# GpSimd sums replanned at their traced length, six weight units as plain float32 products, two additions a pair in batch 1

## The chip, the cores and the metric

The kernel runs on one core of one Trainium2 chip. The metric is the device time of that core in microseconds (us), the median of several runs. One profiled execution of the same program gives the trace from which the rows below come.

## The reference

Softcapped attention over 4 batches, 12 heads, 448 positions and 64 dimensions is followed by two feed-forward networks over the 4 x 448 tokens:

```
scores = cap * tanh((q @ k.T / 8) / cap);  attn = exp(scores - max) / (sum(exp) + 1e-9)
x = (attn @ v) with the heads side by side              # 1792 x 768
h = x @ w_in;  g = 0 if h <= -1, h if h >= 1, else (h + 1)^2 / 4    # 768 -> 2048
y = g @ w_out                                           # 2048 -> 768
out = max(y @ w1, y @ w2, y @ w3) @ w_out2              # 768 -> 768 -> 768
```

The weights come as float64 and are turned into float32 on the chip.

## The kernel before

The work is cut by batch (4) and, in the attention, by pair of heads (6 pairs, `NP`). A pair has 4 chunks (`NCH`) of 112 keys. For each chunk TensorE makes the scores (`score`, L425), ScalarE the tanh (L432); VectorE takes the maximum over the four chunks, GpSimd the maximum over the partitions (`reduce`, L453), VectorE subtracts it from each chunk, ScalarE takes exp (L471), and TensorE multiplies the chunks with v (`weigh`, L619) into the bank `pa`. The sum of the exponentials is formed in one of three ways:

- batch 0: `total` (L485), float32 products of each chunk with ones on TensorE, in four steps a pair;
- batch 1 (`FOURS`): `total4` (L499), for each of the four chunks four products with a 32-column stationary of ones side by side, each over half the columns (224);
- batches 2 and 3 (`POOLED`): three additions a pair on VectorE into `se`, then one GpSimd `partition_all_reduce` into `sb` (L534).

The reciprocal of the sums is taken on 8 partitions: `gather` sends the row into `rc` by a DMA from ScalarE's queue (L575), VectorE inverts, and two DMAs from SyncE's queue spread it into `rs` (only the last pair of batch 0 inverts in place, L607). Then VectorE multiplies: `xf` = `pa` * `rs`. `xf` is split into a high part (L252 or L254) and a rest (L257), both float32r, in the tile `x`.

The feed-forward networks take 64 weight units of 128 x 768 (w_in, w123, w_o2) or 128 x 512 (w_out), in groups that accumulate in a bank `ps_m`. In batch 0 `fetch_first` loads a unit as float64 words into `raw`, and VectorE (L333, L346) and ScalarE (L340) make the float32 unit `wf`, which is stored to DRAM; later batches load it from there (L366). `weights` splits `wf` into high part and rest in `w`. Each product of a 128 x 128 block with a 128 x 448 activation is three float32r matmuls in `parts` (L667 high*high, L668 high*rest, L669 rest*high).

No order is written by hand. Each operation gets a cost for each engine that can do it, a due time (`want`), and the buffers that it uses and takes. `Plan` then runs all of it through a list scheduler and emits each engine's instructions in the order of that plan; the costs are the planner's own and no measurement. Operations of TensorE have a `kind`: a change of kind costs `TURN` = 0.1 and the kind in use is preferred by `STAY` = 3. When a GpSimd operation is planned, VectorE is held for `SHARE` = 1.4. A buffer pool hands out its slots in the order of the due times: `wf` 4, `w` 4, `raw` 3, `h` 9 (for `rs`, `xf` and the tiles of the networks), PSUM banks `m` 3 (`ps_m`, the sums `pr`, and `pa` for the odd pairs of batch 0) and `a` 1. The attention of batch b+1 has due times spread over the networks of batch b, so both are interleaved.

The lines that the change touches most:

```python
PART, SCORE, STEP, SUM = 0.609, 0.8, 0.755, 0.39
ar = op({"P": 2.95}, reduce, w, [m0], [mx], [mb])
ep = op({"P": 2.95}, reduce_sum, begin + 10 + 7 * gap, [sm], [se], [sb])
r = op({"A": 0.6}, gather, w + 0.05, [ep], [src], [rc])
```

Of the kernel before, what the change touches and what calls it, by code (L numbers as in the profile page):

```python
# [20 lines left out]
class Plan:  # L21
# [43 lines left out]
    def run(self):  # L65
# [39 lines left out]
        while left:  # L105
            moved = True
            while moved:
                moved = False
                ts = [o for o in ready if o.kind and at[id(o)] <= t + 1e-9 and can_take(o)]
                turn = min(ts, key=first) if ts else None  # L110

                only = dict.fromkeys(free_at, 0.0)
                for o in ready:
                    if len(o.cost) == 1 and at[id(o)] <= t + 1e-9:
                        e = next(iter(o.cost))
                        only[e] += o.cost[e]
                for o in ready:
                    if at[id(o)] > t + 1e-9 or o.kind and o is not turn:
                        continue
                    idle = [e for e in o.cost if free_at[e] <= t + 1e-9]  # L120
                    if not idle:
                        continue
                    e = next(iter(o.cost))
                    if len(o.cost) > 1:
                        ends = {e: max(free_at[e], t) + only[e] + c for e, c in o.cost.items()}
                        e = min(ends, key=ends.get)
                    if e not in idle or not can_take(o):
                        continue
                    for b in o.takes:
                        free[b.pool] -= 1  # L130
                        queue[b.pool].remove(id(b))
                    c = o.cost[e]
                    if o.kind:
                        c += self.TURN if o.kind != last else 0.0
                        last = o.kind
                    if e == "P":
                        free_at["D"] = max(free_at["D"], t) + self.SHARE
                        heapq.heappush(events, (free_at["D"], serial, None))
                        serial += 1
                    if e == "Q":  # L140

                        free_at[e] = t + c
                        o.t0, o.t1 = t, t + c + 3.2
                    else:
                        free_at[e] = t + c
                        o.t0, o.t1 = t, t + c
                    o.e = e
                    ready.remove(o)
                    done.append(o)
                    heapq.heappush(events, (o.t1, serial, o))  # L150
                    heapq.heappush(events, (free_at[e], serial + 1, None))
                    serial += 2
                    left -= 1
                    moved = True
                    break
            if not left:
                break
            if not events:
                raise RuntimeError("the plan is stuck")
            t = max(t, events[0][0])  # L160
            while events and events[0][0] <= t + 1e-9:
                _, _, o = heapq.heappop(events)
                if o is None:
                    continue
                for b in o.uses:
                    b.users -= 1
                    if not b.users:
                        free[b.pool] += 1
                for x in o.out:
                    x.n -= 1  # L170
                    if not x.n:
                        r = max(
                            d.t1 + (0.0 if d.e in x.cost and len(x.cost) == 1 else self.LATENCY)
                            for d in x.deps
                        )
                        if "Q" in x.cost and x.takes:
                            r = max(r, x.want - self.AHEAD)
                        at[id(x)] = r
                        ready.append(x)
                        serial += 1  # L180
                        heapq.heappush(events, (r, serial, None))
                ready.sort(key=lambda o: key[id(o)])
# [12 lines left out]
def kernel(  # L195
# [23 lines left out]
    NF = w_in.shape[0]  # L219
    NM = w123.shape[1]  # L220
    WU = w_in.shape[2]
    FOURS, POOLED = (1,), (2, 3)

    def pool(name, bufs, **kw):
        return ctx.enter_context(tc.tile_pool(name=name, bufs=bufs, **kw))
# [9 lines left out]
    def buf(p, name, shape, dtype=F32):  # L235
        return plan.buf(p, lambda: pools[p].tile(shape, dtype, tag=p, name=name))
# [133 lines left out]
    def weights(b, i, want):  # L370

        n = width[i]
        wf, got = (fetch_first if b == 0 else fetch_again)(i, want)
        w = buf("w", "w", [P, 2, WU], F32R)
        hi = op(
            c_copy(n / 1000),
            lambda e: copy(e, w.tile[:, 0, :n], wf.tile[:, :n]),
            want - 9, [got], [wf], [w],
        )
        lo = op(  # L380
            c_tt(n / 1000),
            lambda e: tt(
                e, w.tile[:, 1, :n], wf.tile[:, :n], f32(w.tile[:, 0, :n]), ALU.subtract
            ),
            want - 8, [got, hi], [wf, w],
        )
        return w, [hi, lo]


    def attention(b, i, begin, last):  # L390
# [113 lines left out]
            return fn  # L504

        w = begin + 9 + 6 * gap
        if fours or first:
            g = Group(NCH)
            sums = [
                op({"T": SUM if fours else STEP}, (total4 if fours else total)(t[c], g),  # L510
                   w + 0.1 * c, [exps[c]], [t[c], pr], [pr] if c == 0 else [],
                   "sums" if fours else "columns")
                for c in range(NCH)
            ]
            for c in range(1, NCH):
                sums[c].deps.append(sums[0])
        else:
            se = unit("se", rows=C)
            sm = op(
                c_tt(2 * KS),  # L520
                lambda e: tt(e, se.tile, t[0].tile, t[1].tile, ALU.add),
                w, exps[:2], [t[0], t[1]], [se],
            )
            for c in range(2, NCH):
                sm = op(
                    c_tt(2 * KS),
                    lambda e, c=c: tt(e, se.tile, se.tile, t[c].tile, ALU.add),
                    w + 0.1, [sm, exps[c]], [se, t[c]],
                )
            if pooled:  # L530
                sb = unit("sb", rows=C)

                def reduce_sum(e):
                    nc.gpsimd.partition_all_reduce(  # L534
                        out_ap=sb.tile.rearrange("p h s -> p (h s)"),
                        in_ap=se.tile.rearrange("p h s -> p (h s)"),
                        channels=C, reduce_op=bass.bass_isa.ReduceOp.add,
                    )

                ep = op({"P": 2.95}, reduce_sum, begin + 10 + 7 * gap, [sm], [se], [sb])  # L540
            else:
                sums = [op(
                    {"T": STEP}, total(se, Group(1)), begin + 10.9 + 8 * gap, [sm], [se],
                    [pr], "columns",
                )]
        w = begin + 10 + 8.2 * gap

        cols = S // 2 if fours else S
# [14 lines left out]
        if small:  # L563
# [5 lines left out]
            def gather(e):  # L569
                if pooled:  # L570
                    src = sb.tile[0:1].rearrange("p h (c q) -> p (h c) q", q=C)
                else:
                    step = 32 if fours else D
                    src = rs.tile[0:P:step, :cols].rearrange("p (c q) -> p c q", q=C)
                nc.scalar.dma_start(out=rc.tile, in_=src)  # L575

            def spread(e):
                nc.sync.dma_start(out=back, in_=rc.tile)
# [6 lines left out]
                    )  # L585

            src = sb if pooled else rs
            r = op({"A": 0.6}, gather, w + 0.05, [ep], [src], [rc])
            r = op({"S": 3.0 if first else 5.0}, lambda e: None, w + 0.06, [r], [rc, src])

            def turn_over(e):
# [23 lines left out]
        def weigh(c):  # L615
# [10 lines left out]


        avs = [op(
            {"T": STEP}, weigh(0), w, [vl] + (exps[:1] if first else exps + ([] if pooled else sums)),
            [t[0], vt], [pa], "columns",  # L630
        )]
        for c in range(1, NCH):
# [15 lines left out]
            lambda e: tt(e, x.tile[:, 1], xf.tile, f32(x.tile[:, 0]), ALU.subtract),  # L648
            w + 1, [a, hi], [xf, x],
        )  # L650
        return x, [hi, lo]


    def sl(m):
# [1 line left out]

    def parts(pos, want, w, srcs, first, count, ps, g, take):

        wt, wops = w
        done = []  # L660
        for j in range(count):
            a, aops = srcs[first + j]

            def fn(e, j=j, a=a):
                start, stop = g.flags()
                wh, wl = wt.tile[:, 0][:, sl(j)], wt.tile[:, 1][:, sl(j)]
                nc.tensor.matmul(ps.tile[:, :S], wh, a.tile[:, 0], start=start, stop=False)  # L667
                nc.tensor.matmul(ps.tile[:, :S], wh, a.tile[:, 1], start=False, stop=False)  # L668
                nc.tensor.matmul(ps.tile[:, :S], wl, a.tile[:, 0], start=False, stop=stop)  # L669

            o = op(
                {"T": PART}, fn, want(pos + j), [*aops, *wops], [wt, a, ps],
                [ps] if take and j == 0 else [], "layer",
            )
            done.append(o)
        return done
# [176 lines left out]
```

## Time and profile before

| what | value |
|---|---|
| median of 3 runs | 1052.28 us (1052.06 to 1053.23) |
| the profiled execution | 1049.13 us |
| its span, first to last instruction | 1047.3 us |
| TensorE matmuls busy | 1027.1 us, 98% |
| VectorE busy | 812.3 us, 78% |
| ScalarE busy | 508.2 us, 49% |
| GpSimd busy | 154.2 us, 15% |
| mean granted TensorE clock | 0.998 |

Busy time is the union of an engine's instructions; matmuls overlap, each with a tail behind its streaming, so the step from one start to the next is the time that a matmul costs, and the duration in its row is longer. A time in square brackets at the end of a timeline row is how long the engine was idle before it, and who ended the wait.

### The profile page before, as it was taken

The numbers are of one execution on the slowest core, as the hardware profiler recorded it, in microseconds if no ns is written. First come the engines' busy times: TensorE is split into PE (matmuls) and PEld (weight loads), VectorE is DVE, ScalarE is ACT, GpSimd is POOL, SyncE is SP. The second block draws the span as 40 slices with busy tenths as digits, with TensorE's granted clock in tenths as the row PEclk, the third lists the DMA queues.
The fourth block names the chain that finished last, engine by engine and source line by source line (L and its number), as shares of the span: only waits on it lengthen the run. The fifth ranks groups of instructions, "written<-read, shape, count | busy, mean of one in ns | idle before, by whom it ended". The sixth has DMA issues, their size and how long they took to land.

```text
span 1047.3 us, 14331 instructions
## 1 busy us (share of the span) xinstructions
PE 1027.1 (98%) x5472; PEld 813.3 (78%) x5472; DVE 812.3 (78%) x1066; ACT 508.2 (49%) x738; POOL 154.2 (15%) x40
## 2 busy tenths in 40 slices
PE   7988999999999999999999999999999999999998
PEld 2237787787888878878877888788788799999997
DVE  5999999898994889868877589777788578655552
ACT  6887996674571856423523377525235144200101
POOL 2321012011010122132222031231221200000000
PEclk9999999999999999999999999999999999999999
DMA  7339879889885332444234423335432432234331
GB/s 162 123 105 295 280 226 295 290 299 302 285 290 187 99 116 68 119 136 148 96 106 132 146 91 92 108 99 157 126 107 84 143 117 95 91 115 136 106 106 53
DMA packets 66783, 160.53 MB, mean 153 GB/s; under 512 B 8218, under 2 KB 25754, under 8 KB 66714
## 3 DMA queue, kind: packets, MB, share of 16 engines
q1 hardware_dynamic: 66256, 159.53, 48.2%
q8 instruction: 43, 0.70, 0.3%
q14 instruction: 26, 0.21, 0.1%
q10 hardware_dynamic: 458, 0.08, 0.0%
HBM read 131.89 MB, written 27.61 MB: 152 GB/s over the span
## 4 chain that ended last, share of the span: by engine, by line
PE 79%; DVE 7%; DMA 4%; ACT 3%; issue 3%; POOL 3%; SPq 1%; ACTq 0%; POOLq 0%; DVEq 0%
PE ps_m L667 23%; PE ps_m L669 22%; PE ps_m L668 22%; PE ps_s L425 5%; PE ps_a L619 5%; DVE t L257 2%; POOL mb L453 2%; POOL sb L534 1%; DVE mx L257 1%; DMA qk<-in_qk 1%; DVE w L257 1%; PE ps_r L499 1%; ACT t L471 1%; DVE h L750 1%; DMA wf<-w 1%
## 5 line engine op out<-in xcount | busy, mean ns | idle before, releaser
L257 DVE TENSOR_TENSOR w<-wf,w 128x768 fp32r<-128x768 f32 (+1 forms) x256 | 257.1, 1006 | 8.1 <-ACT w L252 4.5
L667 PE MATMUL ps_m<-y,w 128*128 128x448 f32 x432 | 160.4, 371 | 0.0
L254 DVE CAST w<-wf 128x768 fp32r<-128x768 f32 (+1 forms) x120 | 62.5, 521 | 125.2 <-PE ps_m L669 118.7
L668 PE MATMUL ps_m<-y,w 128*128 128x448 f32 x432 | 158.3, 366 | 0.0
L669 PE MATMUL ps_m<-y,w 128*128 128x448 f32 x432 | 158.3, 366 | 0.0
L453 POOL PARTITION_ALL_REDUCE mb<-mx x24 | 79.3, 3306 | 532.7 <-DVE mx L257 424.0
L669 PE MATMUL ps_m<-x,w 128*128 128x448 f32 x384 | 141.4, 368 | 2.9 <-DVE w L257 2.9
L252 ACT ACTIVATE w<-wf 128x768 fp32r<-128x768 f32 (+1 forms) x136 | 101.9, 752 | 86.3 <-PE ps_m L669 60.7
L667 PE MATMUL ps_m<-x,w 128*128 128x448 f32 x384 | 142.8, 372 | 0.0
L667 PE MATMUL ps_m<-g,w 128*128 128x448 f32 x384 | 142.5, 371 | 0.0
L668 PE MATMUL ps_m<-x,w 128*128 128x448 f32 x384 | 141.1, 367 | 0.0
L669 PE MATMUL ps_m<-g,w 128*128 128x448 f32 x384 | 140.5, 366 | 0.0
L668 PE MATMUL ps_m<-g,w 128*128 128x448 f32 x384 | 140.5, 366 | 0.0
L432 ACT ACTIVATE t<-ps_s,qscale 112x896 f32<-112x896 f32 x96 | 92.2, 1003 | 41.9 <-PE ps_s L425 41.9
L471 ACT ACTIVATE t<-t,cap_sb 112x896 f32<-112x896 f32 x96 | 96.5, 1037 | 23.8 <-DVE t L257 23.5
L257 DVE TENSOR_TENSOR t<-t,mb 112x896 f32<-112x896 f32 x96 | 100.1, 1080 | 6.7 <-POOL mb L453 6.7
L667 PEld LDWEIGHTS ps_m<-y,w 128*128 128x128 f32 x432 | 81.1, 188 | 20.3 <-issue 13.4
L425 PE MATMUL ps_s<-qk 64*48 64x448 f32 (+1 forms) x768 | 88.1, 562 | 6.8 <-DMA qk<-in_qk 4.5
L534 POOL PARTITION_ALL_REDUCE sb<-se x12 | 74.7, 6223 | 130.6 <-DVE se L257 118.4
L667 PEld LDWEIGHTS ps_m<-g,w 128*128 128x128 f32 x384 | 72.1, 188 | 18.8 <-issue 10.6
L669 PEld LDWEIGHTS ps_m<-y,w 128*128 128x128 f32 x432 | 81.1, 188 | 7.1
L668 PEld LDWEIGHTS ps_m<-y,w 128*128 128x128 f32 x432 | 81.2, 188 | 6.9
(60 smaller groups left out, 1464.5 us busy)
## 6 DMA issues: line engine op xcount, KB each, us to landing
wf<-w SPq DMA_DIRECT2D x120, 384.0 KB
wf<-w SPq DMA_DIRECT2D x72, 256.0 KB
w<-wf SPq DMA_DIRECT2D x40, 384.0 KB
raw<-in_w SPq DMA_DIRECT2D x18, 768.0 KB
raw<-in_w_in SPq DMA_DIRECT2D x16, 768.0 KB
raw<-in_w_out SPq DMA_DIRECT2D x24, 512.0 KB
qk<-in_qk SPq DMA_DIRECT2D x48, 224.0 KB
w<-wf SPq DMA_DIRECT2D x24, 256.0 KB
```

The lines of the kernel that those rows point to most:

```text
L252: nc.scalar.activation(out=out_, in_=in_, func=AF.Copy)
L254: nc.vector.tensor_copy(out_, in_)
L257: nc.vector.tensor_tensor(out=out_, in0=a, in1=b, op=o)
L425: nc.tensor.matmul(ps.tile[k : k + n, j, :S], qkt.tile[o, 1, c * C + k : c * C + k + n], qkt.tile[o, 0], start=True, stop=True,)
L432: nc.scalar.activation(out=t[c].tile, in_=ps.tile[:C, :, :S], func=AF.Tanh, scale=qscale[:C])
L453: nc.gpsimd.partition_all_reduce(out_ap=mb.tile.rearrange("p h s -> p (h s)"), in_ap=mx.tile.rearrange("p h s -> p (h s)"), channels=C, re ...
L471: lambda e, c=c: nc.scalar.activation(out=t[c].tile, in_=t[c].tile, func=AF.Exp, scale=cap_sb[:C]),
L534: nc.gpsimd.partition_all_reduce(out_ap=sb.tile.rearrange("p h s -> p (h s)"), in_ap=se.tile.rearrange("p h s -> p (h s)"), channels=C, re ...
L619: nc.tensor.matmul(pa.tile[j * D : (j + 1) * D, :S], vt.tile[:, j, c], t[c].tile[:, j], start=start, stop=stop,)
L667: nc.tensor.matmul(ps.tile[:, :S], wh, a.tile[:, 0], start=start, stop=False)
L668: nc.tensor.matmul(ps.tile[:, :S], wh, a.tile[:, 1], start=False, stop=False)
L669: nc.tensor.matmul(ps.tile[:, :S], wl, a.tile[:, 0], start=False, stop=stop)
```

## The change

Four edits. The planner is told that a GpSimd sum takes 6.1 (before 2.95), and `SHARE` is scaled with the length of the GpSimd operation. In batch 0 the first six units of w_in (`PLAIN`) are not split: each product is one float32 matmul of `wf` with `xf`, with a kind and a cost of its own. In batch 1 VectorE adds the chunks by twos (two additions a pair), and `total4` runs over two tiles in place of four. In batches 2 and 3 the DMA of `gather` is issued from SyncE's queue in place of ScalarE's. The due time of the sums in batch 1 moves from `begin + 9 + 6 * gap` to `begin + 10.9 + 8 * gap`.

```diff
-                        free_at["D"] = max(free_at["D"], t) + self.SHARE
+                        free_at["D"] = max(free_at["D"], t) + self.SHARE * c / 3
...
-    FOURS, POOLED = (1,), (2, 3)
+    PLAIN = 6
+    ADDED, FOURS, POOLED = (0, 2, 3, 3), (1,), (2, 3)
...
         wf, got = (fetch_first if b == 0 else fetch_again)(i, want)
+        if b == 0 and i < PLAIN:
+            return wf, [got], True
         w = buf("w", "w", [P, 2, WU], F32R)
...
-        if fours or first:
-            g = Group(NCH)
-            sums = [
-                op({"T": SUM if fours else STEP}, (total4 if fours else total)(t[c], g),
-                   w + 0.1 * c, [exps[c]], [t[c], pr], [pr] if c == 0 else [],
-                   "sums" if fours else "columns")
-                for c in range(NCH)
-            ]
+        if ADDED[b] == 0:
+            srcs = list(zip(t, exps))
+        elif ADDED[b] == 2:
+            srcs = []
+            for c in (0, 2):
+                se = unit("se", rows=C)
+                srcs.append((se, add(t[c], t[c + 1], se, w, exps[c : c + 2])))
         else:
...
-                ep = op({"P": 2.95}, reduce_sum, begin + 10 + 7 * gap, [sm], [se], [sb])
+            ep = op({"P": 6.1}, reduce_sum, begin + 10 + 7 * gap, [sm], [se], [sb])
+        else:
+            g = Group(len(srcs))
+            sums = [
+                op({"T": SUM if fours else STEP}, (total4 if fours else total)(x, g),
+                   (w if first else begin + 10.9 + 8 * gap) + 0.1 * c, [d], [x, pr],
+                   [pr] if c == 0 else [], "sums" if fours else "columns")
+                for c, (x, d) in enumerate(srcs)
+            ]
...
-                nc.scalar.dma_start(out=rc.tile, in_=src)
+                (nc.sync if pooled else nc.scalar).dma_start(out=rc.tile, in_=src)
...
-            r = op({"A": 0.6}, gather, w + 0.05, [ep], [src], [rc])
+            r = op({"Q": 0.1} if pooled else {"A": 0.6}, gather, w + 0.05, [ep], [src], [rc])
...
+            if plain:
+                a, aop = srcs[first + j][2:]
+                aops = [aop]
...
+                if plain:
+                    nc.tensor.matmul(
+                        ps.tile[:, :S], wt.tile[:, sl(j)], a.tile, start=start, stop=stop
+                    )
+                    return
...
-                {"T": PART}, fn, want(pos + j), [*aops, *wops], [wt, a, ps],
-                [ps] if take and j == 0 else [], "layer",
+                {"T": 0.755 if plain else PART}, fn, want(pos + j), [*aops, *wops],
+                [wt, a, ps], [ps] if take and j == 0 else [], "plain" if plain else "layer",
```

## Rows read from the trace of the kernel before

**Rows 1.** Waits of TensorE: who it waited for, total us, times, longest

```profile
PE ps_m L668 <- DVE m L257: 3.2, 2, 1.6
PE ps_m L669 <- DVE w L257: 2.9, 2, 2.2
```

**Rows 2.** Windows: us; busy of PE, PEld, DVE, ACT, POOL; clock; DMA share

```profile
80.00:100.00 20.00, 17.24 (x76) 15.42 (x77) 18.21 (x26) 14.99 (x24) 3.96 (x1) 0.91 0.92 289
...
104.00:320.00 216.00, 215.90 (x1261) 169.15 (x1261) 197.98 (x285) 150.10 (x216) 17.60 (x5) 1.00 0.86 283
320.00:340.00 20.00, 20.00 (x98) 16.12 (x97) 9.29 (x13) 3.19 (x6) 0.00 (x0) 1.00 0.50 167
```

**Rows 3.** Timeline of TensorE, 53 to 104 us: start, length, what

```profile
53.04 0.92 PE L485 MATMUL ps_r<-t,ones 112*64 112x448 f32 x4
53.79 0.92 PE L619 MATMUL ps_a<-t,v 112*64 112x448 f32 x4
...
66.44 0.92 PE L619 MATMUL ps_a<-t,v 112*64 112x448 f32 x4
70.36 0.97 PE L485 MATMUL ps_r<-t,ones 112*64 112x448 f32 x4 [2.99 <-ACT t L471]
...
76.79 0.47 PE L667 MATMUL ps_m<-x,w 128*128 128x448 f32 x1
...
82.42 0.57 PE L667 MATMUL ps_m<-x,w 128*128 128x448 f32 x1
...
85.78 0.38 PE L667 MATMUL ps_m<-x,w 128*128 128x448 f32 x1
...
103.69 0.37 PE L669 MATMUL ps_m<-x,w 128*128 128x448 f32 x1
```

**Rows 4.** Groups by line: busy us, mean ns of one, idle before

```profile
L619 PE MATMUL ps_a<-t,v 112*64 112x448 f32 x384 | 79.4, 544 | 0.0
...
L667 PEld LDWEIGHTS ps_m<-x,w 128*128 128x128 f32 x384 | 72.5, 189 | 16.1 <-issue 9.5 <-DVE w L257 0.7
...
L257 DVE TENSOR_TENSOR se<-se,t 112x896 f32<-112x896 f32 x24 | 26.1, 1086 | 0.8
...
L499 PE MATMUL ps_r<-t,ones 112*32 112x224 f32 x192 | 10.9, 357 | 0.1
```

**Rows 5.** Timeline of VectorE, 65 to 82 us

```profile
65.14 2.33 DVE L346 SCALAR_TENSOR_TENSOR wf<-raw 128x768 int32<-128x768 int32 x1
...
80.08 0.62 DVE L257 TENSOR_TENSOR xf<-ps_a,rs 128x448 f32<-128x448 f32 x1
...
81.09 0.95 DVE L257 TENSOR_TENSOR w<-wf,w 128x768 fp32r<-128x768 f32 x1
81.96 0.62 DVE L257 TENSOR_TENSOR xf<-ps_a,rs 128x448 f32<-128x448 f32 x1
```

**Rows 6.** Timeline of TensorE around one pair's sums in batch 1

```profile
188.81 1.72 PE L499 MATMUL ps_r<-t,ones 112*32 112x224 f32 x32
190.46 0.47 PE L667 MATMUL ps_m<-g,w 128*128 128x448 f32 x1
```

**Rows 7.** Waits of VectorE, 104 to 322 us: who, total us, times, longest

```profile
DVE w L254 <- PE ps_m L669: 4.0, 4, 2.1
```

**Rows 8.** Timeline of GpSimd and of ScalarE around one pooled sum

```profile
615.08 7.04 POOL L534 PARTITION_ALL_REDUCE sb<-se  x1 [11.87 <-DVE se L257]
...
622.88 0.84 ACT L252 ACTIVATE w<-wf 128x768 fp32r<-128x768 f32 x1 [5.06 <-PE ps_a L619]
```

**Rows 9.** Timeline of TensorE in two stretches of float32r matmuls

```profile
591.21 0.37 PE L669 MATMUL ps_m<-x,w 128*128 128x448 f32 x1
...
591.83 0.37 PE L669 MATMUL ps_m<-x,w 128*128 128x448 f32 x1
...
825.15 0.47 PE L667 MATMUL ps_m<-m,w 128*128 128x448 f32 x1
...
1043.33 0.37 PE L669 MATMUL ps_m<-m,w 128*128 128x448 f32 x1
```

More of the change, by code (lines that the diff above doesn't have):

```diff
@@ L386, in weights @@
         )
-        return w, [hi, lo]
+        return w, [hi, lo], False
     def attention(b, i, begin, last):
@@ L506, in attention, with add @@
         w = begin + 9 + 6 * gap
-        if fours or first:
-            g = Group(NCH)
-            sums = [
-                op({"T": SUM if fours else STEP}, (total4 if fours else total)(t[c], g),
-                   w + 0.1 * c, [exps[c]], [t[c], pr], [pr] if c == 0 else [],
-                   "sums" if fours else "columns")
-                for c in range(NCH)
-            ]
-            for c in range(1, NCH):
-                sums[c].deps.append(sums[0])
+        def add(x, y, out, w, deps):
+            return op(
+                c_tt(2 * KS), lambda e: tt(e, out.tile, x.tile, y.tile, ALU.add),
+                w, deps, [x, y, out], [] if out is x else [out],
+            )
@@ L517, in attention @@
+        if ADDED[b] == 0:
[5 more added lines that the diff above has]
+                srcs.append((se, add(t[c], t[c + 1], se, w, exps[c : c + 2])))
         else:
             se = unit("se", rows=C)
[L519 to L523, printed above, removed]
@@ L524, in attention @@
-            for c in range(2, NCH):
[L525 to L528, printed above, removed]
-                )
[L530 to L538, printed above, removed]
-                ep = op({"P": 2.95}, reduce_sum, begin + 10 + 7 * gap, [sm], [se], [sb])
[L541 to L545, printed above, removed]
+            sm = add(t[0], t[1], se, w, exps[:2])
@@ new lines, in attention, with reduce_sum @@
+            for c in range(2, NCH):
+                sm = add(se, t[c], se, w + 0.1, [sm, exps[c]])
+            srcs = [(se, sm)]
+        if pooled:
+            sb = unit("sb", rows=C)
+            def reduce_sum(e):
+                nc.gpsimd.partition_all_reduce(
+                    out_ap=sb.tile.rearrange("p h s -> p (h s)"),
+                    in_ap=se.tile.rearrange("p h s -> p (h s)"),
+                    channels=C, reduce_op=bass.bass_isa.ReduceOp.add,
+                )
+            ep = op({"P": 6.1}, reduce_sum, begin + 10 + 7 * gap, [sm], [se], [sb])
[7 more added lines that the diff above has]
+            ]
+            for c in range(1, len(srcs)):
+                sums[c].deps.append(sums[0])
@@ L628, in attention @@
         avs = [op(
-            {"T": STEP}, weigh(0), w, [vl] + (exps[:1] if first else exps + ([] if pooled else sums)),
+            {"T": STEP}, weigh(0), w,
+            [vl] + (exps[:1] if first else exps if pooled else exps + sums),
             [t[0], vt], [pa], "columns",
@@ L650, in attention @@
         )
-        return x, [hi, lo]
+        return x, [hi, lo], xf, a
     def sl(m):
@@ L657, in parts @@
     def parts(pos, want, w, srcs, first, count, ps, g, take):
-        wt, wops = w
+        wt, wops, plain = w
         done = []
         for j in range(count):
-            a, aops = srcs[first + j]
+            a, aops = srcs[first + j][:2]
+            if plain:
+                a, aop = srcs[first + j][2:]
+                aops = [aop]
             def fn(e, j=j, a=a):
                 start, stop = g.flags()
+                if plain:
+                    nc.tensor.matmul(
+                        ps.tile[:, :S], wt.tile[:, sl(j)], a.tile, start=start, stop=stop
+                    )
+                    return
                 wh, wl = wt.tile[:, 0][:, sl(j)], wt.tile[:, 1][:, sl(j)]
```

## The prediction

> **What bounds the kernel now.** I read the waits of TensorE first, then the windows, then TensorE's timeline where the windows show it idle. From 104 us to the end TensorE is all but never idle: in the window from 104 to 320 us it is busy for 215.90 of 216 us [rows 2], and later it waits only twice, 1.6 us each time, for the last split at the end of a batch [rows 1]. So behind 104 us only two things can move the end: the number and price of TensorE's own steps, and a new wait. Ahead of 104 us there is slack. TensorE stands for 2.99 us before the last pair's columns, then begins the networks at 76.79 us, waits 2.9 us in two places for the rest part of a weight unit [rows 1, 3], and for a while gets the lower of its two clock levels (1.2 GHz against 2.4): the clock row says 0.91 for 80 to 100 us [rows 2]. The sixth unit of w_in ends there: 6 units x 6 products x 3 matmuls are 108 matmuls, from 76.79 us to 103.69 us plus one step, 103.9 us [rows 3].
>
> VectorE is the second engine to watch: 197.98 us busy of 216 in the stage where batch 0's networks and batch 1's attention run together, then only 9.29 of 20 [rows 2].
>
> **Part 1: the plain products.** A float32r product is three steps. In one stretch the same line returns after 0.62 us [rows 9]; in the other, 825.15 to 1043.33 us holds 1,077 steps of 0.2026 us, and three of them are 0.608. A full 128 x 128 float32 matmul does not occur in the trace. Its nearest rows: L619 shows 544 ns for one instruction where a float32r matmul over the same 448 columns shows 0.37 us [rows 4, 9]; 0.17 us more is nearly one more step of 0.2026, so a float32 instruction streams its columns at half the speed. L499, with 224 columns, shows 357 ns [rows 4], as it should if half the columns at half the speed. The trace also holds two instructions for each float32 matmul: 384 L619 instructions stand for 24 pairs x 4 chunks x 2 heads = 192. One step of four instructions, two heads on two halves of the columns, takes 53.79 - 53.04 = 0.75 us [rows 3]. A full-width product uses the whole array for the same two instructions, so I take 0.755. Bounds: 0.41 (two steps at float32r speed, which the 544 ns speaks against) and 1.13, if the weight loads are not hidden: a full-width load shows 189 ns [rows 4], and a product has two. Against the upper end: a float32r step takes 0.2026 us, less than its load and its streaming one after the other, so loads do run under the matmul before them. The Trainium skill, "TensorE: Matmul & The Clock Gate", Part 3 (The mechanism), says that a weight load overlaps a running matmul only when the row group differs; by that rule the upper end would hold, and the sum would come to 1060.5. The trace disagrees for float32r, whose loads and matmuls all use the same 128 rows; for a full-width float32 product no row here shows it. Price: 36 x (0.755 - 0.609) = **+5.3 us**.
>
> What it takes away: the split of six units, on VectorE 6 x 0.95 = 5.7 us [rows 5] and as many high parts on ScalarE. TensorE's 2.9 us of waits for L257 fall, since plain products need only `wf` and `xf`. So does, I think, the lower clock, which follows upon those waits: from 82.42 to 85.78 us nine steps take 3.36 us, 0.373 each against 0.203, that is 1.5 us [rows 3]. Together **-4.4 us**.
>
> What it may fill: `wf` of unit 0 is ready at 65.14 + 2.33 = 67.5 us [rows 5], and four `xf` exist by then or soon after; the hole from 67.4 to 70.36 us takes up to four products of 0.755. A limit stands behind it. Three banks `m` serve `ps_m`, the last pair's `pr` and its `pa`; so with unit 0 and unit 1 open, no third unit starts until the last `xf`, and TensorE waits for the fifth `xf`, at 80.08 + 0.62 = 80.7 us [rows 5]. Worked as a sequence with the hole filled: columns end at 76.9 us, unit 1 with four `xf` to 79.9, a wait to 80.7, the fifth `xf` for both units to 82.2, the sixth (81.96 us before, some 0.9 earlier without the L257 of 81.09) to 83.7, then 24 products to 101.8 us: 2.1 earlier than 103.9. With the hole unfilled: units 0 and 1 to 82.8, then the rest, 103.9: nothing won. The list decides which; the due time of unit 0 lies behind those of the columns, but a free TensorE takes what is ready. I take **-1.5 us** for all of part 1, with -2.1 and +5.3 (all dearer products on the path, the waits merely moved) as ends. The `xf` now hold six of nine `h` slots until then; the three left serve six units at 4.5 us each, and I price that at nothing, since a `ps_m` bank can wait for one unit's length.
>
> **Part 2: two additions a pair in batch 1.** Four `total4` take 190.46 - 188.81 = 1.65 us of TensorE [rows 6], 0.41 each. Two a pair go, 12 in all: 12 x 0.41 = **-4.9 us**, in a stage where TensorE has no idle time. Ends: -4.6 (a fixed part of each visit stays) and -5.2 (pairs whose sums were cut in two visits lose one). VectorE gets 12 additions at 1.086 us [rows 4], 13.0 us. From 104 to 320 us it has 216 - 198 = 18 us idle, of which 4.0 are waits for TensorE [rows 2, 7]; another 10.7 us are idle from 320 to 340, and the 5.7 us of part 1 leave VectorE ahead when the stage begins. 104 to 340 us asks for 207 + 13 = 220 us of VectorE in about 230. That fits, but with 4% to spare, in order, so some unit or `g` comes late: I take **+1.0 us**, ends 0 and 9.0 (13.0 less the 4.0 that were plain waiting for TensorE).
>
> **Part 3: GpSimd replanned, `gather` on SyncE's queue.** The sum took 7.04 us in one place, and ScalarE stood 5.06 us until just after its end, because the gather's DMA waits in its queue [rows 8]. That wait goes from ScalarE, which has idle time there; TensorE did not wait. On SyncE's queue the loads of later `wf` stand behind the same DMA. With the sum planned at 6.1 the gather is placed later in the list, so the wait there should be about a microsecond, against units that are split three to four units (3.65 us each) ahead. Zero, with ends -3.2 (both end-of-batch waits [rows 1] fall into better places) and +2 (a load too late).
>
> **Sum.** -1.5 - 4.9 + 1.0 + 0 = -5.4 us. The profiled execution took 1049.13 us, so it would take 1043.7. The median of the timed runs is 3.15 us above it; I carry that over: 1052.28 - 5.4 = **1046.9 us**. 0.2% (2.1 us) is about what a measurement of this kernel can tell from no change.
>
> **The rivals.**
> (a) The dearer products land on the path whole: no hole filled, and the waits come back as waits for the last two `xf`. +5.3 - 4.9 + 1.0 = +1.4: 1053.7. For it: the bank limit; against: 7 us of idle or slow time stand there.
> (b) VectorE becomes the bound of batch 0's networks. The additions cost their upper end: -1.5 - 4.9 + 9.0 = +2.6: 1054.9, slower. For it: 92% busy; against: the idle stretch behind 320 us. It decides as soon as TensorE waits more than 8.5 us for VectorE between 104 and 340 us.
> (c) The pace of the float32r steps flips. Stretches of the same matmuls run at 0.2026 or at 0.2067 (0.62 / 3) [rows 9], one pace held through a stretch, and the order of the other work may set which. The last stretch, 1,077 steps, has the quick pace: losing it costs 1,077 x 0.0041 = 4.4: 1051.3. The other way, if some 1,200 slow steps turn quick, 4.9 are won: 1042.0.
> (d) The weight loads of a full-width float32 matmul are not hidden: 2 x 0.189 for each of 36 products are 13.6 us: -5.4 + 13.6 = +8.2: 1060.5, slower. It decides from 0.1 us a load, where the 36 products cost 7.2 us more.
> (e) The replan moves the two end-of-batch waits away: -5.4 - 3.2: 1043.7.
>
> **How the numbers follow.** The forecast has a chance of 0.56, (a) 0.12, (b) 0.08, (c) 0.10 slow and 0.06 quick, (d) 0.02, (e) 0.06. Faster: 0.56 + 0.06 + 0.06 = 0.68; within 0.2%: (a) and slow (c), 0.22; slower: (b) and (d), 0.10. The range from 1041.5 to 1053.8 takes in (a), (c) and (e) and leaves out 0.10 and the edges; the forecast's own is 1043.5 to 1050.
>
> **What would show it.** A plain product from start to start at 0.75 us; the 36th ending near 102 us, without a wait for L257 ahead of it and without a stretch at the lower clock; 16 instructions of L499 a pair, about 0.8 us; TensorE's waits for VectorE between 104 and 340 us at about a microsecond; SyncE, not ScalarE, waiting for `sb`. The prediction is wrong if a plain product costs 0.9 us or more, if TensorE waits on VectorE in batch 0's networks, or if the pace of the last stretch changes.

## The result and the profile after

The changed kernel takes 1039.87 us (median of 5 runs, 1039.19 to 1040.71), against 1052.06 us for the kernel before beside it (1049.29 to 1053.23): ratio 0.989, 95% interval 0.9876 to 0.9904. Measured a second time it was 1039.78 against 1049.86: 0.9906, interval 0.9891 to 0.9921. The change is faster, by 10 to 12 us, about twice the 5.4 us forecast; 1046.9 us was predicted and 1041.5 was the low end. The profiled execution takes 1040.38 us, its span 1038.6 us; from profile to profile 8.7 us are gone.

TensorE's waits after the change (who it waited for, total us, times, longest):

```profile
PE ps_s L430 <- DMA qk<-in_qk: 4.2, 1, 4.2
PE ps_r L490 <- ACT t L476: 2.6, 4, 1.2
PE ps_s L430 <- ACT t L437: 2.2, 8, 0.4
PE ps_m L683 <- DVE y L260: 1.4, 1, 1.4
```

Both lines of [rows 1] are gone: the waits for the rest part of a weight unit in the first stage, and the two for the split of `m` at the ends of batches 1 and 2. One new wait stands there, 1.4 us for the split of `y` in batch 0's networks. The windows that answer to [rows 2]:

```profile
80.00:100.00 20.00, 20.00 (x55) 9.83 (x54) 19.59 (x27) 14.76 (x24) 3.96 (x1) 1.00 0.97 317
...
104.00:320.00 216.00, 214.32 (x1186) 168.44 (x1185) 200.04 (x282) 152.96 (x225) 14.86 (x5) 1.00 0.87 283
320.00:340.00 20.00, 20.00 (x116) 16.27 (x114) 9.65 (x15) 5.31 (x9) 0.00 (x0) 1.00 0.57 186
```

From 80 to 100 us TensorE is never idle and the granted clock is 1.00, not 0.91. TensorE's timeline around the plain products, which answers to [rows 3]:

```profile
67.34 1.02 PE L677 MATMUL ps_m<-xf,wf 128*128 128x448 f32 x2
69.58 0.97 PE L490 MATMUL ps_r<-t,ones 112*64 112x448 f32 x4 [1.22 <-ACT t L476]
...
74.52 1.02 PE L677 MATMUL ps_m<-xf,wf 128*128 128x448 f32 x2
...
77.12 26.02 PE L677 MATMUL ps_m<-xf,wf 128*128 128x448 f32 x68
102.63 0.71 PE L682 MATMUL ps_m<-x,w 128*128 128x448 f32 x1
```

Two instructions are one product. One stands in the hole at 67 us (TensorE's idle time ahead of the last pair's columns), one at 74.5 us, and 34 run from 77.12 to 102.63 us without a break: 25.51 / 34 = 0.750 us each. Before, the same 36 products ended at 103.9 us.

Where the 8.7 us come from can be read off three marks, TensorE's first step of a stage: the first product of batch 1's networks stands at 332.57 us (338.37 before), that of batch 2's at 581.03 (588.93), that of batch 3's at 830.51 (839.25). So 5.8 us come before batch 1's networks, 2.1 in the first batch end, 0.8 in the second, where the wait taken away was worth 1.6 and slower float32r steps took some back; behind it nothing (208.05 us before, 208.09 after).

### The profile page after: what moved, and what is told of

It reads as the page before. It is cut to its first block, busy times and chain, and to the rows that moved or that the text cites. A ratio compares the mean times of both kernels' runs of the same rounds, so it can differ in the third digit from the quotient of the medians.

```text
span 1038.6 us, 14098 instructions
## 1 busy us (share of the span) xinstructions
PE 1024.6 (99%) x5340; PEld 803.1 (77%) x5340; DVE 805.1 (78%) x1049; ACT 516.7 (50%) x755; POOL 150.8 (15%) x40
## 4 chain that ended last, share of the span: by engine, by line
PE 77%; ACT 0%; issue 0%; ACTq 0%; DVE 0%
PE ps_m L682 23%; PE ps_m L683 22%; PE ps_m L684 22%; PE ps_a L625 5%; PE ps_s L430 4%; PE ps_r L504 0%; ACT o L255 0%; ACTq L255 0%; DVE w L260 0%
## 5 line engine op out<-in xcount | busy, mean ns | idle before, releaser
L260 DVE TENSOR_TENSOR w<-wf,w 128x768 fp32r<-128x768 f32 (+1 forms) x250 | 242.1, 970 | 8.0 <-ACT w L255 5.0
L257 DVE CAST w<-wf 128x768 fp32r<-128x768 f32 (+1 forms) x109 | 57.1, 524 | 133.6 <-PE ps_m L684 129.3
L255 ACT ACTIVATE w<-wf 128x768 fp32r<-128x768 f32 (+1 forms) x141 | 105.9, 754 | 104.3 <-PE ps_m L684 84.3
L682 PE MATMUL ps_m<-x,w 128*128 128x448 f32 x348 | 129.2, 371 | 0.0
L683 PE MATMUL ps_m<-x,w 128*128 128x448 f32 x348 | 127.3, 366 | 0.0
L684 PE MATMUL ps_m<-x,w 128*128 128x448 f32 x348 | 127.3, 366 | 0.0
L535 POOL PARTITION_ALL_REDUCE sb<-se x12 | 72.4, 6035 | 137.0 <-DVE se L260 57.3
```

Source lines behind the costliest of these rows:

```text
L255: nc.scalar.activation(out=out_, in_=in_, func=AF.Copy)
L257: nc.vector.tensor_copy(out_, in_)
L260: nc.vector.tensor_tensor(out=out_, in0=a, in1=b, op=o)
L535: nc.gpsimd.partition_all_reduce(out_ap=sb.tile.rearrange("p h s -> p (h s)"), in_ap=se.tile.rearrange("p h s -> p (h s)"), channels=C, re ...
```

## The experiments

All differences below are of medians, in us, against 1039.8, the changed kernel measured twice (ten executions, 1038.41 to 1040.71). Each kernel was measured beside the kernel before, and the ratio to it is given too. The kernel before varies by several us, so these intervals are wide, and for the smaller differences below they overlap that of the changed kernel; such a difference rests on the times alone. The times of different measurements can be set side by side: from the first product of batch 3's networks to the end, every profile takes 208.0 to 208.1 us, but for one with a wait there (208.9).

**The kernel before, profiled again, twice.** No edit.

> The kernel before, unchanged, profiled once more, because its profiled execution took 1049.13 us and most of its timed ones about 1052. Theory A (the pace of the float32r steps differs from one execution to the next): if this execution is near 1052, some of its stretches that ran at 0.2027 us a step run at 0.2067 now, some 700 steps more, and its waits are the same. Theory B (a wait that comes and goes): the paces by stretch are the same, and about 3 us more stand in a wait or in the stretch before 104 us.

> The kernel before, profiled a third time. Theory B (its executions differ by waits of TensorE between 60 and 340 us, at the same places or near them, and not by the pace): the time behind 340 us, from the first product of batch 1's networks to the end, agrees within 1 us with the first profile (1047.3 - 338.4 = 708.9 us), and the rest of the difference stands before 340 us. Theory A (the pace): the part behind 340 us differs by 2 us or more.

The first took 1054.27 us (span 1052.5), the second 1049.03 (span 1047.2). Waits of TensorE from 77 to 340 us, in the slower one (6.9 us in all, against 3.1 in the quicker one):

```profile
PE ps_m L669 <- DVE w L257: 4.1, 2, 2.2
PE ps_s L425 <- ACT t L432: 1.8, 1, 1.8
PE ps_m L668 <- DVE y L257: 0.8, 1, 0.8
PE ps_r L499 <- ACT t L471: 0.2, 1, 0.2
```

Batch 1's networks begin there at 343.14 us, in the quicker one at 337.81. From that mark to the end it is 1052.5 - 343.1 = 709.4, 1047.2 - 337.8 = 709.4, and 708.9 us in the first profile. Theory B holds for where the difference arises: ahead of the mark. Waits make 3.8 of its 5.3 us, TensorE's lower clock 1.4: in the slower execution the granted clock falls twice, after the idle time that ends at 69.58 us and after the wait that ends at 97.16 us, in the quicker one once, near 82 us. The same steps, from the end of that idle time to the first product, take 77.44 - 69.58 = 7.86 us in the one and 75.88 - 69.45 = 6.43 in the other. Behind the mark the three sums agree, but not their parts: the slower execution gets the lower clock again (0.373 us a step) after a wait of 1.97 us at the end of batch 2, and more of its other steps have the quick pace there.

```profile
821.31 0.47 PE L668 MATMUL ps_m<-m,w 128*128 128x448 f32 x1 [1.97 <-DVE m L257]
...
822.16 0.57 PE L668 MATMUL ps_m<-m,w 128*128 128x448 f32 x1
...
825.41 0.36 PE L668 MATMUL ps_m<-m,w 128*128 128x448 f32 x1
```

VectorE is busy for 198 of 216 us in the stage ahead of the mark [rows 2]; that a few us of waiting fall out differently there each time for this reason is argued, not shown.

**Without the replan.**

```diff
-self.SHARE * c / 3
+self.SHARE
-ep = op({"P": 6.1}, reduce_sum, ...
+ep = op({"P": 2.95}, reduce_sum, ...
```

> The changed kernel with the planner's old figures: a GpSimd sum planned at 2.95, VectorE held for 1.4 whatever the length. Theory 1 (the replan took away the two waits of 1.6 us at the ends of batches 1 and 2): both waits are back, the median is 3.3 us above the changed kernel's, about 1043.2. Theory 2 (the waits went because the other parts moved the order of the list): no such wait, the median within 1 us of 1039.9.

1043.78 us, +4.0 (ratio to before 0.9939, interval 0.9923 to 0.9954), and both waits are back in its profile. The granted clock was 1.000 in that execution and 0.998 in the other five, so part of what the 4.0 us hold above the waits may be the lower clock.

```profile
PE ps_m L683 <- DVE m L260: 3.2, 2, 1.6
```

**The replan alone**, the same two figures changed in the kernel before.

> The kernel before with the planner's new figures alone (6.1 for the sum, VectorE's hold scaled with the length). Theory 1 (the two waits at the ends of batches 1 and 2 are a matter of these figures alone): no wait of TensorE for the split of m in either place, and 3.3 us faster than the kernel before, ratio 0.997. Theory 2 (it needs the other parts): the waits stay, ratio 1.000.

1046.08 us against 1049.86: 0.996, interval 0.9942 to 0.9979. No wait for the split of `m` is left; TensorE's waits in its profile behind 77 us are one line:

```profile
PE ps_m L669 <- DVE w L257: 2.6, 2, 1.9
```

So theory 1 both ways: two planner's figures, not a single instruction more or less, are worth some 4 us (1049.86 - 1046.08 = 3.8, and 4.0 the other way).

**Without the plain products** (`PLAIN = 0`).

> The changed kernel with no plain products in batch 0 (PLAIN = 0). Theory 1 (part 1 is worth what the end of the 36th product moved, 1.3 us): 1041.2, and the waits of TensorE for VectorE after 104 us stay under 2 us. Theory 2 (what counts is that VectorE is relieved of six splits before the twelve additions come): TensorE waits 3 us or more for VectorE between 77 and 340 us, and the median is at 1044 or more.

1044.18 us, +4.4 (0.9944, interval 0.9929 to 0.9959). Theory 2: TensorE waits 5.6 us for VectorE from 77 to 340 us, and batch 1's networks begin at 336.08 us in place of 332.57.

```profile
PE ps_m L684 <- DVE w L260: 4.9, 5, 1.9
...
PE ps_r L504 <- DVE y L260: 0.7, 1, 0.7
```

The lower clock is back with the waits: the granted clock (third number from the end) from 60 to 104 us, first here, then in the changed kernel:

```profile
60.00:104.00 44.00, 39.26 (x184) 25.92 (x180) 41.03 (x54) 33.08 (x48) 7.10 (x2) 0.92 0.70 217
```

```profile
60.00:104.00 44.00, 42.75 (x156) 18.34 (x153) 43.42 (x55) 32.08 (x46) 7.10 (x2) 1.00 0.72 228
```

All six executions without plain products have 0.997 or 0.998 over the whole time, the ten of the changed kernel 0.999 or 1.000, those of the kernel before 0.994 to 0.998. So theory 2 counts one thing too few: the plain products take away waits and the lower clock that came after them.

**Without the additions in batch 1** (`ADDED = (0, 0, 3, 3)`).

> The changed kernel with four total4 a pair in batch 1 again and no additions there (the due time of the sums stays the new one). Theory 1 (the sums' steps are 4.9 to 5.3 us of TensorE, and VectorE's additions cost TensorE some 2 us of waits): 3 us slower, 1042.9, and the wait of 1.4 us for the split of y at 229 us is gone. Theory 2 (VectorE had room for the additions, the wait at 229 us has another cause): 5 us slower, 1044.9, with the wait still there.

1046.07 us, +6.3 (0.9957, interval 0.9943 to 0.9972); the wait at 229 us is gone, 0.6 us for a weight unit is all that TensorE still waits for VectorE. More than either theory: the sums' steps, 4.5 (9.9 us here, 5.4 in the changed kernel), and the pace of the float32r steps, 1.7: from 104 us to batch 1's networks the slower pace costs 2.2 us here and 0.5 in the changed kernel (steps added up above 0.2027 us). With the replan alone (1046.08), and with these two runs, four kernels cover additions and plain products: neither 1046.1, plain products alone 1046.1, additions alone 1044.2, both 1039.8. Each alone is worth 0 and 1.9 us, both together 6.3. With the pace in that stretch taken out it is 0.6, 1.2 and 5.2: still more together than apart. (The first kernel also lacks the move of the gather's queue, for which the next run finds no gain, and the new due time of the sums, which was not tried by itself.)

**The gather on ScalarE's queue again.**

```diff
-(nc.sync if pooled else nc.scalar).dma_start(out=rc.tile, in_=src)
+nc.scalar.dma_start(out=rc.tile, in_=src)
-r = op({"Q": 0.1} if pooled else {"A": 0.6}, gather, ...
+r = op({"A": 0.6}, gather, ...
```

> The changed kernel with the gather's DMA of batches 2 and 3 on ScalarE's queue again, all else kept. Theory 1 (the queue is off the path: TensorE waited for nothing there): within 0.8 us of the changed kernel, though ScalarE waits some 5 us for sb in places. Theory 2 (a ScalarE that waits for sb delays the split of m at the batch ends, so the queue is part of the gain): one or both end-of-batch waits are back, 1.6 to 3.3 us slower.

1038.17 us against 1039.78 of the changed kernel beside it; the intervals of the ratios 0.9900 (0.9884 to 0.9915) and 0.9906 (0.9891 to 0.9921) overlap. Its orders on TensorE and GpSimd are those of the changed kernel; VectorE's and ScalarE's differ from 367 us on. Its profile is 2.7 us quicker: 2.0 before 330.6 us, where the two kernels are the same, and 1.0 in batch 2's networks, where more float32r steps have the quick pace. No wait came back at the batch ends: the queue is off the path, and the edit shows no gain.

**Three additions a pair** (`ADDED = (0, 3, 3, 3)`), **and the same with the gather on ScalarE's queue.**

> The changed kernel with three additions a pair in batch 1 and one total4: six total4 fewer, six additions of 1.08 us more. Theory 1 (VectorE still has room in batch 0's networks, as its waits there say): about 0.44 x 6 = 2.6 us faster, 1037.3. Theory 2 (VectorE is at its limit with two): TensorE's waits for VectorE between 104 and 340 us grow by 3 us or more, and the time is the same or slower.

> Three additions a pair in batch 1, one total4, and the gather on ScalarE's queue: the quickest of the versions so far put together. TensorE has 2.6 us fewer steps than in the changed kernel; if the waits for VectorE in batch 0's networks are a matter of the execution and not of the third addition, 1037.3; if VectorE is at its limit, 1039 to 1040.

1039.86 us, the same as the changed kernel (0.9911, 0.9898 to 0.9924), and 1039.07 us for the second (0.9885, 0.986 to 0.991). Neither theory holds. Six steps of `total4` less are 2.3 us (5.4 to 3.1) and bring batch 1's networks to 330.81 us, 1.8 earlier; TensorE's waits up to there sum to 2.2 us in place of 1.7, but those for VectorE are 1.1, no more than the 1.4 of the changed kernel. Another 0.8 us is lost in batch 3's networks, where TensorE waits 0.5 us for a split of `x`. No version was shown to be quicker than the changed kernel.

**The splits of the plain units done all the same**, into tiles that no product reads: the early return moves behind the two splits.

```diff
-        if b == 0 and i < PLAIN:
-            return wf, [got], True
         w = buf("w", "w", [P, 2, WU], F32R)
...
+        if b == 0 and i < PLAIN:
+            return wf, [got], True
         return w, [hi, lo], False
```

> The changed kernel with its plain products, but the first six units are split all the same into tiles that no product reads: six high parts (0.84 us) and six rests (0.95 us on VectorE) come back as idle work, TensorE's steps stay those of the changed kernel. Theory 1 (part 1 is worth mostly the work that it takes from VectorE and ScalarE ahead of the twelve additions): the waits of TensorE between 77 and 340 us come back, 4 to 6 us, and the median is at 1043 to 1044.5, near that of the kernel without plain products. Theory 2 (it is worth what TensorE no longer has to wait for, since plain products need no split): within 1 us of the changed kernel.

1044.43 us, +4.6 (0.9935, 0.991 to 0.996): as slow as without plain products. Theory 1, though TensorE's waits came back to 3.1 us only, and its profile has a stretch at the lower clock behind one of them. But the planner reckons with the twelve instructions, so load and order changed together. Two more kernels part them: in one the twelve are emitted and planned at 0.0001, in the other planned at their cost and not emitted.

> The changed kernel in which the six plain units are split all the same into tiles that no product reads, and the planner is told that these twelve instructions cost nothing: TensorE's order is the changed kernel's, instruction by instruction, and VectorE and ScalarE have 5.7 and 5.0 us more to do. Theory 1 (the load itself costs: the added work comes when VectorE is at its limit, and TensorE waits): 4 us slower than the changed kernel, about 1044, TensorE's waits between 77 and 340 us above 4 us. Theory 2 (the order that the planner makes for the extra work costs): within 1 us of the changed kernel.

> The other half: the planner reckons with the six splits, but nothing is emitted for them; the order is that of the kernel with idle splits, the load that of the changed kernel. Theory 1 (load): within 1 us of the changed kernel. Theory 2 (order): 1043 to 1044.5.

The load alone gives 1043.92 us, +4.1 (0.9925, 0.9898 to 0.9952; six executions, 1042.78 to 1045.0); the order alone 1041.78, +2.0 (0.9902, 0.9878 to 0.9926; 1040.76 to 1042.11). With the order of TensorE unchanged, the load brings these waits between 77 and 340 us:

```profile
PE ps_m L684 <- DVE w L260: 1.4, 1, 1.4
PE ps_m L677 <- DVE xf L260: 1.0, 1, 1.0
PE ps_s L430 <- ACT t L437: 0.9, 1, 0.9
PE ps_m L683 <- DVE y L260: 0.8, 1, 0.8
```

They sum to 4.1 us where the changed kernel has 1.7, and batch 1's networks begin 3.2 us later; the granted clock is 1.00 up to there, so this loss needs no lower clock. Mostly the load, then; part of the loss is the planner's order, and the two do not add up (4.1 + 2.0 against 4.6). (The idle splits also take slots of the pool `w`; that share was not parted from the load.)

**Three and nine plain units** (`PLAIN = 3`, `PLAIN = 9`).

> The changed kernel with three plain units in place of six: 18 products go back to three float32r steps, 18 x 0.142 = 2.6 us less of TensorE's steps, and three splits more on VectorE. Theory 1 (relief of VectorE): TensorE waits some 2 us more for VectorE before 340 us, so the median is within 1 us of the changed kernel. Theory 2 (plain products only cost): 2.6 us faster, 1037.2.

> The changed kernel with nine plain units: 18 more dear products, 2.6 us more of TensorE's steps, three splits fewer. Only some 1.5 us of waits for VectorE are left between 77 and 340 us to be won. Theory 1: 1 to 2.6 us slower, 1040.8 to 1042.4. Theory 2 (the h slots held by xf longer stall the networks): a new wait, more than 2.6 us slower.

1041.14 us, +1.3 (0.9905, 0.988 to 0.993; 1040.86 to 1041.83), and 1042.0 us, +2.2 (0.9909, 0.9887 to 0.9932; 1040.82 to 1042.33). With three, TensorE waits 2.9 us for weight units again; with nine it waits for nothing between 77 and 340 us, and pays the 18 x (0.750 - 0.609) = 2.5 us of dearer products, which puts batch 1's networks 0.8 us later; another 1.1 us of its profile is the slower pace of float32r steps in batch 1's networks. Of the three numbers tried six is the quickest, by little; there was no stall from the `h` slots.

## Why the prediction was wrong in size, point by point

**The end of each batch: the step that failed.** Part 3 was priced at zero, with -3.2 as its end and 0.06 as the chance of rival (e). It measures 3.2 us in waits and 3.8 to 4.0 us in medians. I had weighed the gather's queue, which shows no gain, and not what the planner does with VectorE. At the end of batch 1 the last GpSimd sum runs just when the last `m` must be split. VectorE and GpSimd before, timelines:

```profile
561.22 5.96 POOL L534 PARTITION_ALL_REDUCE sb<-se  x1 [10.83 <-DVE se L257]
```

```profile
561.85 0.62 DVE L257 TENSOR_TENSOR top<-ps_m,top 128x448 f32<-128x448 f32 x1
562.61 3.96 DVE L257 TENSOR_TENSOR w<-wf,w 128x768 fp32r<-128x768 f32 x1
566.49 0.61 DVE L257 TENSOR_TENSOR m<-top,m 128x448 fp32r<-128x448 f32 x1
```

and after:

```profile
555.79 5.39 POOL L535 PARTITION_ALL_REDUCE sb<-se  x1 [11.24 <-PE ps_m L684]
```

```profile
556.37 4.20 DVE L260 TENSOR_TENSOR w<-wf,w 128x768 fp32r<-128x768 f32 x1
560.49 0.61 DVE L260 TENSOR_TENSOR m<-top,m 128x448 fp32r<-128x448 f32 x1
```

In both a weight split (0.95 us elsewhere) is held to 4 us while the sum runs, and the split of `m` stands behind it. That did not change. What changed is TensorE's order. Its timeline before, from the last network's first product on `m` to the wait, and after, from that product to the last matmul that starts before the split ends:

```profile
561.49 0.37 PE L667 MATMUL ps_m<-m,w 128*128 128x448 f32 x1
...
567.16 0.47 PE L668 MATMUL ps_m<-m,w 128*128 128x448 f32 x1 [1.59 <-DVE m L257]
```

```profile
555.63 0.37 PE L682 MATMUL ps_m<-m,w 128*128 128x448 f32 x1
...
561.00 0.37 PE L684 MATMUL ps_m<-m,w 128*128 128x448 f32 x1
```

Before, TensorE stands for the split after 19 matmuls. After, no matmul up to 563.78 us waits, although the split ends at 561.1 us: at least 27 matmuls stand ahead of the first that needs it. The kernel with the replan alone shows it by itself: the sum takes 5.96 us and the split begins 5.0 us after the first product on `m` (566.95 against 561.95 us), both as before, and 28 matmuls start before the split ends, none of them waiting. Told that VectorE is held for 1.4 x 6.1 / 3 = 2.85 and not 1.4, the planner puts products that do not need the split first; which ones moved was read from these counts, not tried. The row agrees with the Trainium skill, "SBUF — State Buffer" (Who interferes with whom): a VectorE instruction with two SBUF inputs contends with a GpSimd instruction that reads SBUF. The subtraction of two SBUF tiles took 4.20 us in place of 0.95, while the maximum with one operand in PSUM took its usual 0.62 us during the sum before. For VectorE's two-port modes the page says that whoever issues first holds the shared ports for the whole instruction and the other blocks; here VectorE's instruction ended 0.6 us before the sum's recorded end, and recorded spans on GpSimd are rough.

**The base: the second step that failed.** I carried the 3.15 us between the profiled execution and the median over to the new kernel. They were no fixed overhead: executions of the kernel before run from 1047.71 to 1057.9 us and their medians from 1049.86 to 1052.06, the profiled one was among the quicker, and three executions gave the median that I took. Where its profiles differ in time, they differ by waits and by the lower clock before 340 us. The changed kernel's two profiles have 1.7 us of such waits each and no lower clock in that time: it has little to lose there. Its profile (1040.38) and its median (1039.87) agree. From profile to profile the sum of -5.4 stands beside -5.8 before batch 1's networks and -2.9 net at the batch ends: 1049.13 - 8.7 = 1040.4, and 1040.38 is what it took. The rest of the median's gain, 3.4 us measured first and 1.3 measured again, is this base.

**Part 1: the price right, the worth mis-read.** A plain product takes 0.750 us (0.755 taken), the 36th ends 1.3 us earlier (1.5 taken), there is no wait for a split ahead of it and no stretch at the lower clock. The hole took one product and not four; a second went in before the last pair's last chunk. Rival (d) fell: a full-width load shows 190 ns and lies wholly under the matmuls.

```profile
L677 PE MATMUL ps_m<-xf,wf 128*128 128x448 f32 x72 | 28.1, 545 | 0.0
...
L677 PEld LDWEIGHTS ps_m<-xf,wf 128*128 128x128 f32 x72 | 13.3, 190 | 14.7 <-issue 12.4 <-DVE xf L260 1.1 <-DVE wf L349 0.7
```

With loads not hidden, a product would have taken the 1.13 us of the prediction's upper bound. A sentence of the Trainium skill, "TensorE: Matmul & The Clock Gate", Part 3 (The mechanism), lets loads overlap running matmuls only when the row group differs, though the section also lets the background weight buffer be loaded ahead. The 0.750 us for two instructions on the same 128 rows disagree with that sentence for float32, as the rows did for float32r.

But the 1.3 us is not what the edit is worth. Taken out, it costs 4.4 us; with its splits done idly, 4.1 to 4.6; without the additions, nothing, or 0.6 with the pace taken out. It pays by taking 5.7 us from VectorE and 5.0 from ScalarE just before the additions put 13.0 on VectorE, and by sparing TensorE the lower clock; how the 4.4 us divide between the two was not parted.

**Part 2: right, and only because of part 1.** A pair's sums now take 16 instructions and 0.90 us to the next start:

```profile
234.07 0.96 PE L504 MATMUL ps_r<-se,ones 112*32 112x224 f32 x16
234.97 0.60 PE L625 MATMUL ps_a<-t,v 112*64 112x448 f32 x2
```

Over six pairs that is 5.4 us, in six visits, against 10.5 in eight before, 5.1 us less (4.9 taken). The waits for VectorE that come in are 1.4 us (1.0 taken). Rival (b), VectorE as the bound, is what the kernel without plain products shows: 5.6 us of waits, short of the 8.5 from which the sum would have turned. Behind the plain products, batch 1's networks come 4.5 us nearer where 3.9 was forecast. Of the 4.5, 1.1 is the pace of float32r steps (1.5 us lost to the slower one before, 0.5 after), for which the sum had no term: that -5.4 and -5.8 lie so close is in part luck.

**Rival (c)**, the pace, came out even over the whole: stretches turned both ways, up to batch 3's networks the slower pace cost 5.0 us in both kernels, and the last stretch kept the quick pace in every run here.

## What to carry to other kernels

In a kernel ordered by a planner, a wrong cost for an engine that is hardly busy can sit on the path of the busiest one: look at what its operations hold up elsewhere, at each place where the order leaves the critical engine without other work. Where a second engine is within a few per cent of its limit, price edits in pairs: here relief and added load there were worth 0 and 1.9 us apart and 6.3 together. When a wait of TensorE is taken away, look whether the granted clock fell after it: the lower clock then goes with the wait. And before a profiled execution's distance to the median is carried over, find out in which stage it arises; a distance made of waits goes when the waits go.

## What the runs showed that was not expected

The same program's executions differ by up to 5.3 us ahead of one mark (batch 1's networks begin between 337.81 and 343.14 us in three profiles of the kernel before) and agree within 0.5 us in the 709 us behind it, with different parts. A wait of 2 us can cost more than itself: the steps behind it at the lower clock were another 1.4 to 1.6 us. Float32r steps of one form run at 0.2027 or 0.2067 us, one pace held through a stretch, the longest of 1,077 matmuls; from 104 us to batch 1's networks the slower pace cost 0.5 us in one kernel and 2.2 in another, and much the same each time in profiles of one kernel (0.5 and 0.6; 1.3 to 1.5). What sets it stays open.
